# Sixteen output stores made as two halves each, and four departures of a written-out order changed, in an attention and MLP kernel on one core

## The chip, the cores and the metric

One core of one Trainium2 chip runs the kernel. The metric is the device time of one execution in microseconds; the shown time is the median of three runs. Engines are named as the profile names them: PE is the matrix engine (PEld its weight loads), DVE the vector engine, ACT the scalar engine, POOL GpSimd and SP the sync engine, which issues most of the DMAs here. Each engine runs its own list of instructions in order, and they wait for each other by semaphores.

## The reference, cut to what matters

```python
def _attn_ref(x, inducing):            # x: 4 x 12544 x 128, inducing: 32 x 128
    def mab(q, kv):
        s = scale * (q @ kv.transpose(0, 2, 1))
        s = s - s.max(-1, keepdims=True)
        a = np.exp(s)
        a /= a.sum(-1, keepdims=True) + 1e-09
        return a @ kv
    h = mab(I, x)                      # 32 rows that attend to all of x, for each batch
    return mab(x, h)                   # each row of x attends to these 32

def _moe_ref(x, w1, w2, w_out):        # 50176 x 128, 128 x 1024 twice, 1024 x 128
    h1 = x @ w1
    h2 = x @ w2
    g = np.maximum(h1, h2)
    return g @ w_out
```

The attention's output is the input of the second part. x and the output are float32, 25.7 MB each.

## The kernel before, in words

**Tiling.** A batch is cut into 98 chunks of 128 rows (`K = 98`). Row `98 p + k` of a batch lies in partition `p` of chunk `k`, so that `m` chunks that follow each other are `m` times 512 bytes in a row of memory for each partition. The four batches follow each other. For each batch the 32 pooled rows `h` are summed first (`pool_scores`, `pool_turn`, `pool_accum`, and the `small_...` functions), while the batch before is in its main part.

**Main part.** max(h1, h2) is taken as h1 + relu(h2 - h1), so one linear term and one relu term are needed. A `Block` holds up to four quarters of up to four chunks each; a quarter lives in 32 partitions. `stage` makes a block's scores (L610) and their exponentials `e`. `phase` (matmuls at L1069) sends up to four jobs at once through the four 32-row strips of PE: relu units, each one PSUM bank of 512 columns, which ACT (L1085) or DVE (L1088) then takes through the relu into SBUF, or the linear term of a group. `final_one` (L876) is one matmul of 128 columns that adds relu(h2 - h1) times `w_out` to a group's bank. A `Group` is up to four chunks of one quarter and has eight such matmuls for each chunk.

**Eviction and store.** When a group's last matmul is issued, `evict_group` multiplies the bank by the reciprocal of the softmax sums on DVE (L907) into an output tile `o`, of which there are six in turn (`outp`, `bufs=6`), and stores it at once (L935). Chunks that lie side by side go out in one DMA; four chunks are 256 KB. All stores but the last group's are issued by SP, the last one by ACT. In six groups of batch 2 (56, 60, 64, 68, 72, 76 in the order of groups) the store is already made as two DMAs of half the chunks. In the compiled program each DMA takes one of eight landing semaphores in turn, and an instruction that needs a buffer again waits for the landings of the DMAs that used it.

**SP's list.** Besides the stores, SP issues the DMA transposes of x (L172), of the pooling exponentials (L366), and, for the blocks from number 21 on, of `e` for the softmax sums (L688), which POOL then adds up (L698, L700). At the end of the program SP waits for all DMAs (L1315), and the engines leave together.

**The order.** A planner in the kernel walks through steps with a clock of its own (`Clock`) and decides at each step between a phase and a final matmul. Where the order was changed by hand, the table `DEV` names the step and the departure: 1 holds a ready phase back for one final matmul, 2 lets a phase go earlier, 3 lets a phase go ahead of column work, 4 lets column work go ahead. The table's keys are step numbers, so a change at one step shifts the meaning of the ones behind it unless they are made to fit again.

Of the kernel before, what the change touches and what calls it, by code (L numbers as in the profile page):

```python
# [102 lines left out]
def kernel(  # L103
# [93 lines left out]
    with tc.manual_schedule(engines={ET.PE, ET.DVE, ET.Activation, ET.Pool, ET.SP}):  # L197
# [585 lines left out]
        groups, ends = [], [0] * 4  # L783
# [5 lines left out]
        groups = [g for _, _, g in sorted(groups, key=lambda e: e[:2])]  # L789
# [55 lines left out]
        def linear_last(end):  # L845

            while held:
                g = held[0]
                if g.full:
                    if st[g.blk.b].get("m1r", INF) > ck.pe:  # L850
                        return
                    for s, (q, t) in enumerate(g.chunks):
                        nc.tensor.matmul(  # L853
                            out=g.ps[:, 128 * s : 128 * (s + 1)],
                            lhsT=g.blk.e2[:, 128 * t : 128 * (t + 1)],
                            rhs=m1bd[:, q, :],
                            start=False,
                            stop=True,
                            skip_group_check=True,
                        )  # L860
                    end = ck.run(0.056 * len(g.chunks))
                evict_group(held.pop(0), end)
# [30 lines left out]
        def evict_group(g, end):  # L893
            n = len(g.chunks)
            while g.blk.rp is None:
                f, a = next(job for job in pending if job[0] in DEN and job[1][0] is g.blk)
                pending.remove((f, a))
                f(*a)
            uid[0] += 1
            osb = outp.tile([128, 4, C], F32, name=f"o_{uid[0]}", tag="o")  # L900
            qs = sorted({q for q, _ in g.chunks})
            per = n // len(qs)
            t0 = g.chunks[0][1]
            rp = g.blk.rp[:, t0 : t0 + per, qs[0] : qs[-1] + 1]
            if len(qs) == 1:
                rp = rp.broadcast_to((128, per, C))
                nc.vector.tensor_mul(osb[:, 0:n, :], g.ps[:, 0 : n * C].rearrange("p (s c) -> p s c", s=n), rp)  # L907
            elif per == 1:
                rp = g.blk.rp[:, t0, qs[0] : qs[-1] + 1]
                nc.vector.tensor_mul(  # L910
                    osb[:, 0:n, :],
                    g.ps[:, 0 : n * C].rearrange("p (s c) -> p s c", s=n),
                    rp[:, :, None].broadcast_to((128, n, C)),
                )
            else:
                for i, q in enumerate(qs):
                    nc.vector.tensor_mul(
                        osb[:, per * i : per * (i + 1), :],
                        g.ps[:, per * i * C : per * (i + 1) * C].rearrange("p (s c) -> p s c", s=per),
                        g.blk.rp[:, t0 : t0 + per, q : q + 1].broadcast_to((128, per, C)),  # L920
                    )
            ck.bank[g.bank] = ck.on_dve(end, 0.066 + n * 128 / 960.0)
            runs = []
            for s, (q, t) in enumerate(g.chunks):
                qu = g.blk.quarters[q]
                c = qu.c0 + t
                if runs and runs[-1][0] == qu.b and runs[-1][1] + runs[-1][3] == c:
                    runs[-1][3] += 1
                else:
                    runs.append([qu.b, c, s, 1])  # L930
            queue = nc.scalar if g is groups[-1] else nc.sync
            for b, c, s, m in runs:
                h = m // 2 if groups.index(g) in (56, 60, 64, 68, 72, 76) else m
                for lo in range(0, m, h):
                    queue.dma_start(out=outr[b, :, c + lo : c + lo + h, :], in_=osb[:, s + lo : s + lo + h, :])  # L935
            chunks_done[0] += n
# [23 lines left out]
        def want_linear():  # L960
# [32 lines left out]
        }  # L993
        LIMIT = -16

# [324 lines left out]
```

## Time and profile before

| | |
|---|---|
| median of three runs | 324.81 us (324.77, 324.81, 325.58) |
| the profiled execution | 325.08 us |
| its span, first to last instruction | 323.2 us, granted clock 1.00 |
| DMA packets | 75,016, 53.99 MB, 167 GB/s over the span |
| HBM read and written | 27.28 MB and 25.69 MB |
| SP's own longest wait | 27.8 us, a store for its eviction |

A line of a group gives the source line, the engine, the operation, what it writes and reads, its count, then busy time, mean of one, and idle time before. `L935` is line 935 of the kernel. The chain is followed back from the last instruction through what released each step; its shares are of the span. In a table of stretches each row begins with from:to in microseconds and gives an engine's busy time with its number of instructions. In a row of a DMA queue stand packets, megabytes and the time that the packets took as a share of 16 DMA engines over the stretch. A line of waits gives engine and line, whom it waited for, the sum in us, how often and the longest. Landing is counted from the issue to the completion of a DMA.

### The profile page before, as it was taken

What the parts mean: (1) busy time and instruction counts of PE and PEld (TensorE: products, weight loads), DVE (VectorE), ACT (ScalarE), POOL (GpSimd) and SP (SyncE); (2) the same over time, 40 slices, a digit from 0 to 9 for tenths busy, and PEclk for the clock granted to TensorE, in tenths of its full rate; (3) what the DMA queues carried; (4) which work ended last, traced back from release to release, by engine and by line L of the source; (5) the groups of instructions that cost most, each with busy time, mean ns of one, the idle gap of its engine ahead of it and who ended that gap; (6) DMA issues with size and microseconds to landing.
All of it is one profiled execution on the core that took longest, in us unless ns stands there. A gap on an engine that the chain in (4) does not pass through costs nothing.

```text
span 323.2 us, 12580 instructions
## 1 busy us (share of the span) xinstructions
PE 315.9 (98%) x5375; PEld 240.1 (74%) x5375; DVE 281.3 (87%) x508; ACT 281.7 (87%) x561; POOL 37.8 (12%) x90
## 2 busy tenths in 40 slices
PE   7899999999999999999999999999999999999995
PEld 3776777777777777777777777777777777777785
DVE  3369999988989998999989999988989999899973
ACT  3789999998978999999898999998879999999960
POOL 7470000000040000000040000000006300402000
PEclk9999999999999999999999999999999999999999
DMA  8999999975279999894289999693324312323232
GB/s 205 207 267 213 226 247 199 204 137 130 99 161 243 221 249 210 161 206 145 100 163 240 232 245 191 152 228 111 118 99 109 138 67 100 125 99 116 100 115 100
DMA packets 75016, 53.99 MB, mean 167 GB/s; under 512 B 55856, under 2 KB 60624, under 8 KB 74960
## 3 DMA queue, kind: packets, MB, share of 16 engines
q1 hardware_dynamic: 68928, 39.42, 50.2%
q0 software_dynamic: 5888, 13.70, 21.7%
q8 instruction: 42, 0.69, 0.9%
q14 instruction: 14, 0.11, 0.1%
q10 hardware_dynamic: 144, 0.07, 0.1%
HBM read 27.28 MB, written 25.69 MB: 164 GB/s over the span
## 4 chain that ended last, share of the span: by engine, by line
PE 92%; DMA 5%; ACT 1%; issue 1%; POOL 0%; DVE 0%; POOLq 0%
PE ps L876 62%; PE ps L1069 22%; DMA xn<-in_x_dram 5%; PE ps L610 2%; PE ps L385 2%; PE ps L329 1%; PE ps L671 1%; PE ps L833 1%; ACT e L629 0%; PE ps L505 0%; ACT hwd L482 0%; PE ps L235 0%; PE ps L303 0%; PE ps L430 0%; PE ps L258 0%
## 5 line engine op out<-in xcount | busy, mean ns | idle before, releaser
L1085 ACT ACTIVATE relu<-ps 128x512 f16<-128x512 f32 x462 | 244.1, 605 | 23.0 <-PE ps L1069 15.0
L1088 DVE TENSOR_SCALAR relu<-ps 128x512 f16<-128x512 f32 x322 | 205.9, 681 | 16.3 <-PE ps L1069 15.0
L876 PE MATMUL ps<-woutp,relu 128*128 128x128 f16 x3136 | 216.8, 220 | 0.0
L876 PEld LDWEIGHTS <-relu 128*128 128x128 f16 x3136 | 176.6, 98 | 39.5 <-issue 28.9
L1069 PE MATMUL ps<-e,hwd 32*128 32x512 f16 (+2 forms) x888 | 88.2, 358 | 0.1
L907 DVE TENSOR_TENSOR o<-ps,rp 128x512 f32<-128x512 f32 (+3 forms) x80 | 51.1, 639 | 1.8 <-PE ps L876 1.3
L1069 PEld LDWEIGHTS <-hwd 32*128 32x128 f16 x888 | 24.5, 91 | 20.9 <-issue 0.8
L1069 PE MATMUL ps<-m,e 32*128 32x128 f16 x381 | 38.7, 217 | 0.0
L1069 PEld LDWEIGHTS <-e 32*128 32x128 f16 x381 | 21.2, 92 | 2.9 <-issue 0.4
L907 DVE TENSOR_TENSOR o<-ps,rpt 128x512 f32<-128x512 f32 (+3 forms) x28 | 17.3, 617 | 4.1 <-PE ps L853 2.2
L166 POOL DMA_DIRECT2D xn<-in_x_dram x33 | 17.9, 553 | 6.5 <-DMA xn<-in_x_dram 4.4
L164 POOL COPY pace<-hacc 128x1 f32<-128x1 f32 x2 | 0.4, 188 | 133.0 <-DVE hacc L418 133.0
L246 DVE COPY xT<-ps 128x768 f16<-128x768 f16 (+6 forms) x11 | 4.7, 457 | 8.8 <-PE ps L235 8.8
L340 ACT ACTIVATE eu<-ps 128x512 f16<-128x512 f32 x18 | 10.9, 616 | 0.1
L629 ACT ACTIVATE e<-ps 128x512 f16<-128x512 f32 (+2 forms) x21 | 10.4, 570 | 0.2 <-PE ps L610 0.2
L235 PE MATMUL ps<-identity,xn 128*128 128x128 f16 x98 | 8.6, 228 | 1.8 <-DMA xn<-in_x_dram 1.7
L535 POOL COPY m1bd<-m 32x128 f16<-32x128 f16 x4 | 1.1, 287 | 76.7 <-DVE m L530 76.6
L249 ACT COPY xT<-ps 128x768 f16<-128x768 f16 (+5 forms) x10 | 6.5, 672 | 2.9 <-PE ps L235 2.8
L698 POOL TENSOR_TENSOR w1T<-den 128x256 f32<-128x256 f16 (+1 forms) x7 | 4.4, 631 | 38.2 <-DMA den<-e 24.8
L700 POOL TENSOR_TENSOR w1T<-w1T 128x64 f32<-128x64 f32 (+4 forms) x28 | 8.4, 301 | 2.2
L235 PEld LDWEIGHTS <-xn 128*128 128x128 f16 x98 | 6.0, 102 | 3.4 <-DMA xn<-in_x_dram 2.1
L610 PE MATMUL ps<-xT,hT 128*32 128x512 f16 (+3 forms) x114 | 8.2, 361 | 0.0
(93 smaller groups left out, 117.0 us busy)
## 6 DMA issues: line engine op xcount, KB each, us to landing
out_dram<-o SPq DMA_DIRECT2D x84, 256.0 KB, 2.4
xn<-in_x_dram POOLq DMA_DIRECT2D x24, 448.0 KB, 10.1
out_dram<-o SPq DMA_DIRECT2D x22, 128.0 KB, 2.1
wf<-in_moe_w_dram POOLq DMA_DIRECT2D x4, 256.0 KB, 6.0
xn<-in_x_dram POOLq DMA_DIRECT2D x3, 224.0 KB, 8.8
xT<-xn SPq DMA_TRANSPOSE x42, 4.0
xf<-in_x_dram SPq DMA_DIRECT2D x1, 512.0 KB, 3.6
xf<-in_x_dram SPq DMA_DIRECT2D x1, 384.0 KB, 4.1
```

The costliest lines, as they stand in the source:

```text
L166: nc.gpsimd.dma_start(out=xn_at[b, i][lo:hi, 0:n, :], in_=xr[b, lo:hi, k0 : k0 + n, :])
L235: nc.tensor.transpose(ps[:, j, :], xn_at[0, i][:, g + j, :], identity16)
L249: nc.scalar.copy(out=dst, in_=ps[:, 0:m, :])
L340: nc.scalar.activation(out=eu, in_=ps, func=AF.Exp, scale=scale, accum_out=st[b]["es"][:, u : u + 1])
L610: nc.tensor.matmul(out=ps[32 * q : 32 * (q + 1), 128 * t : 128 * (t + n)], lhsT=hq, rhs=xT[:, c : c + n, :], start=True, stop=True, tile_p ...
L629: nc.scalar.activation(out=blk.e2[:, lo:hi], in_=ps[:, lo:hi], func=AF.Exp, scale=st[0]["rs"] if blk.b == 0 else scale,)
L700: nc.gpsimd.tensor_add(acc[:, :, 0:n], acc[:, :, 0:n], acc[:, :, n : 2 * n])
L876: nc.tensor.matmul(out=g.ps[:, 128 * c : 128 * (c + 1)], lhsT=g.blk.relu[q][:, 128 * (jb * w4 + t) : 128 * (jb * w4 + t + 1)], rhs=woutp[: ...
L907: nc.vector.tensor_mul(osb[:, 0:n, :], g.ps[:, 0 : n * C].rearrange("p (s c) -> p s c", s=n), rp)
L1069: nc.tensor.matmul(**seq[i])
L1085: nc.scalar.activation(out=dst, in_=src, func=AF.Relu)
L1088: nc.vector.tensor_scalar(out=dst, in0=src, scalar1=0.0, scalar2=None, op0=ALU.max)
```

## The change

Two edits. In `evict_group` the pieces of a store are two chunks long where the store has four chunks and its group is one of the six of before or one of the groups 78 to 94; all other stores stay whole. Sixteen stores of batch 3 come out as two DMAs of 128 KB in place of one of 256 KB. In the table `DEV` the entries 1409, 1413, 1442 and 1451 go, and 1425, 1431, 1438, 1440 and 1447 come in.

```diff
             for b, c, s, m in runs:
-                h = m // 2 if groups.index(g) in (56, 60, 64, 68, 72, 76) else m
+                h = 2 if m == 4 and (groups.index(g) in (56, 60, 64, 68, 72, 76) or 78 <= groups.index(g) < 95) else m
                 for lo in range(0, m, h):
                     queue.dma_start(out=outr[b, :, c + lo : c + lo + h, :], in_=osb[:, s + lo : s + lo + h, :])
...
-            1371: 2, 1386: 1, 1390: 4, 1403: 3, 1407: 4, 1409: 1, 1413: 3, 1420: 1, 1434: 1, 1442: 1, 1451:
-            4, 1454: 1, 1461: 2, 1467: 2, 1476: 3, 1480: 1, 1486: 1, 1492: 1, 1496: 1, 1507: 1, 1521: 1,
...
+            1371: 2, 1386: 1, 1390: 4, 1403: 3, 1407: 4, 1420: 1, 1425: 1, 1431: 1, 1434: 1, 1438: 2, 1440:
+            1, 1447: 3, 1454: 1, 1461: 2, 1467: 2, 1476: 3, 1480: 1, 1486: 1, 1492: 1, 1496: 1, 1507: 1,
```

The other lines of the table are only broken anew. In the compiled program SP has 16 instructions more and DVE 9 (waits for landings); ACT, POOL and PE have as many as before. PE's order differs in three places near 153 us, which the prediction names; every other engine's work keeps its order.

10 rows, old and new, of the table DEV are left out of this document.

## The prediction

> **What bounds the kernel now.** I read the page first, then busy time by stage, then the last microseconds: waits of the sync engine (SP), time to landing, and DMA packets by queue.
>
> ```profile
> span 323.2 us, 12580 instructions
> ...
> PE 315.9 (98%) x5375; PEld 240.1 (74%) x5375; DVE 281.3 (87%) x508; ACT 281.7 (87%) x561; POOL 37.8 (12%) x90
> ...
> q8 instruction: 42, 0.69, 0.9%
> q14 instruction: 14, 0.11, 0.1%
> q10 hardware_dynamic: 144, 0.07, 0.1%
> ...
> PE 92%; DMA 5%; ACT 1%; issue 1%; POOL 0%; DVE 0%; POOLq 0%
> ```
>
> The matrix engine (PE) carries 92% of the chain that ended last. Two rows matter below: queues 8 and 14 carry no data but the engines' own code. 0.69 MB for PE's 5375 + 5375 instructions is 64 bytes each, and a fetch on queue 14 is 0.11 MB / 14, 8 KB, so 128 instructions. The busy times of the stages that the edited stores lie in, 257 to 305 us, and on both sides of it:
>
> ```profile
> 230.00:257.00 27.00, 27.00 (x494) 20.87 (x490) 24.31 (x48) 23.18 (x45) 8.66 (x24) 1.00 0.35 110
> 257.00:305.00 48.00, 48.00 (x779) 36.62 (x776) 45.32 (x78) 45.45 (x89) 5.18 (x15) 1.00 0.29 102
> 305.00:320.00 15.00, 14.56 (x265) 12.93 (x263) 10.61 (x21) 7.34 (x14) 0.00 (x0) 1.00 0.33 120
> ```
>
> Columns: length, then PE, weight loads, DVE, ACT, POOL, then clock, DMA share and GB/s. PE is busy 48.00 of 48.00 us: nothing that the stores do there can make PE faster, only slower. What is left to gain lies behind PE's last matmul. The end, from the timeline and the stores' landing times (window 318 to the end):
>
> ```profile
> 318.89 0.61 PE L876 MATMUL ps<-woutp,relu 128*128 128x128 f16 x8
> ...
> 319.10 0.79 DVE L907 TENSOR_TENSOR o<-ps,rpt 128x256 f32<-128x256 f32 x2 [0.45 <-PE ps L853]
> ...
> 319.92 0.37 ACTq L935 DMA_DIRECT2D out_dram<-o  x1
> ```
>
> ```profile
> L935 SPq DMA_DIRECT2D out_dram<-o x2: 332/332/332, 318.7 to 319.5; - x2
> L935 ACTq DMA_DIRECT2D out_dram<-o x1: 370/370/370, 319.9 to 319.9; - x1
> ...
> DMA to landing us min/median/max: 1.7/1.8/2.4
> ```
>
> ```profile
> SPq L1315 <- DMA out_dram<-o: 1.6, 2, 1.0
> ```
>
> The last store goes out on ACT's queue at 319.92 and is the only one of 64 KB among the three. The two larger ones on SP's queue land in 1.7 and 1.8 us; this one, the smallest, takes 2.4. SP waits at the end of the program for both of the last landings, 1.0 us for the longer, and only then do the engines leave. So the last store's landing sets the end, and it is 0.6 to 0.7 us slower than its neighbours. DMA packets show why (four windows: 320.80:321.12, 321.12:321.14, 321.15:321.47, 321.47:321.70):
>
> ```profile
> q10 hardware_dynamic: 132, 0.06, 64.5%
> ...
> q14 instruction: 1, 0.01, 110.3%
> q10 hardware_dynamic: 2, 0.00, 11.2%
> ...
> q10 hardware_dynamic: 1, 0.00, 0.2%
> ...
> q10 hardware_dynamic: 9, 0.00, 6.1%
> ```
>
> Queue 10 is this one store: 144 packets on the page, 9 for each of 16 DMA engines. 132 start before 321.12 and 3 more by 321.15; then none for 0.32 us; then exactly 9, one engine's whole share, one after the other. In the gap lies one packet on queue 14, a code fetch at 321.13. Its time is 110.3% of 16 engines over 0.02 us, 0.35 us. One DMA engine was given an 8 KB code page first, and the last store had to wait for it.
>
> **Whose fetch it is.** From 320.3 to 321.13 only SP moves on, with one drain of ACT beside it:
>
> ```profile
> L1315 SPq EVENT_SEMAPHORE  x6: 28/28/28, 320.3 to 320.6; - x6
> ```
>
> SP's instructions between the fetch at 98.80 us (window 98.75:98.85 holds one packet of queue 14) and 321.13, first and last groups of nine:
>
> ```profile
> q14 instruction: 1, 0.01, 19.3%
> ...
> L935 SPq DMA_DIRECT2D out_dram<-o x88: 332/334/1971, 102.1 to 319.5; - x88
> L935 SPq EVENT_SEMAPHORE  x81: 17/17/17, 103.8 to 319.1; - x81
> ...
> L1315 SPq EVENT_SEMAPHORE  x7: 28/28/28, 319.9 to 320.6; - x7
> ```
>
> With the 42, 24 and 14 of the three kinds of transposes and their waits between them, the nine groups sum to 256, two pages of 128 exactly. So I read the fetch at 321.13 as SP's, and its place as a count of SP's instructions.
>
> **The change part by part, and its cost.**
>
> *Sixteen stores become two each.* Rows of the page for both sizes:
>
> ```profile
> out_dram<-o SPq DMA_DIRECT2D x84, 256.0 KB, 2.4
> ...
> out_dram<-o SPq DMA_DIRECT2D x22, 128.0 KB, 2.1
> ```
>
> Bytes stay the same. SP gets 16 more issues of 0.33 us (the store rows above), 5.3 us in all, in a stage of 48 us in which it waits 26.1 us for evictions:
>
> ```profile
> SPq L935 <- DVE o L907: 26.1, 12, 3.6
> ```
>
> The halves land about as the wholes do. Six output buffers at one store per 48/17 = 2.8 us give 17 us before a buffer is written again. Landing times of 2 to 2.4 us lie far inside that, so I take 0. Without that cover an eviction would wait the second issue, at most 0.33 us, and PE perhaps after it.
>
> *The 16 more instructions move SP's fetch.* All stand ahead of SP's last 16 instructions before 321.13. These are (window 313 to 321.13):
>
> ```profile
> L935 SPq DMA_DIRECT2D out_dram<-o x5: 332/332/333, 313.8 to 319.5; - x5
> L935 SPq EVENT_SEMAPHORE  x4: 17/17/17, 314.2 to 319.1; - x4
> ```
>
> with the 7 waits at L1315 above, 16 together. So the page ends in front of the store at 313.8, behind the one at 312.2, and the fetch should start about 0.5 us after the wait between them (as 321.13 stands to the last wait at 320.6): near 313 us. There it delays at most a share of the store of 312.2 by 0.35 us; that store's buffer is next needed, six evictions on, by the last eviction, whose group starts at 319.10. Cost 0. The last store then finds all 16 DMA engines free. The gain: at least the fetch's 0.35 us, at most 2.4 - 1.7 = 0.7. All nine packets of the late engine came behind the fetch, so without it they run beside the others', which had all started by 321.15; I take the upper part, 0.65 us.
>
> [...]
>
> *DVE gets 9 more waits.* An eviction that reuses a split buffer now waits for two landings, which takes 9 more wait instructions in the compiled list of DVE. Before, from 190 to 238 us, where six stores are split already, and from 257 to 305:
>
> ```profile
> L907 DVEq EVENT_SEMAPHORE  x17: 21/21/50, 190.5 to 235.6; - x17
> L907 DVE TENSOR_TENSOR o<-ps,rp x16: 679/680/691, 191.6 to 236.2; 128x512 f32<-128x512 f32 x16
> ...
> L907 DVEq EVENT_SEMAPHORE  x17: 21/50/50, 258.5 to 303.9; - x17
> L907 DVE TENSOR_TENSOR o<-ps,rpt x17: 676/680/692, 259.1 to 304.4; 128x512 f32<-128x512 f32 x17
> ```
>
> A wait is 0.02 to 0.05 us. Evictions take 680 ns with both kinds, so the waits pass while DVE still works on the operation before. Bounds 0 and 9 x 0.05 = 0.45 us; what would be late is the next relu, and behind it PE, for DVE is busy 45.3 of 48 us. I take 0.
>
> *The departures.* PE's list keeps its 10,739 rows and every switch; near 153 us three runs of L876 change from 3, 13, 13 to 4, 11, 14 matmuls (the run of 13 between them stays):
>
> ```profile
> 152.63 0.33 PE L876 MATMUL ps<-woutp,relu 128*128 128x128 f16 x3
> ...
> 153.22 0.90 PE L876 MATMUL ps<-woutp,relu 128*128 128x128 f16 x13
> ...
> 155.54 0.90 PE L876 MATMUL ps<-woutp,relu 128*128 128x128 f16 x13
> ...
> 156.71 0.96 PE L876 MATMUL ps<-woutp,relu 128*128 128x128 f16 x14
> ```
>
> 29 matmuls before and after. One more is 0.96 - 0.90 = 0.06 us, so a phase comes 0.06 later or earlier. If a bank is late the loss is at most the 0.12 that the run of 11 is shorter; at best 0.06 of a wait goes. Value 0. Relus on ACT and DVE keep their order.
>
> *Sum.* The profiled execution took 325.08 us, its span 323.2 and 1.9 around it. 325.08 - 0.65 = 324.43. The runs shown have a median of 324.81 (324.77 to 325.58), 0.27 less; carried over, 324.81 - 0.65 = 324.16.
>
> **The rivals.**
> 1. *No gain.* [...] Time 324.8. Chance 0.17.
> 2. *Half.* The last store is late of itself, as the first on its queue, and only the fetch's own 0.35 us goes: 324.46. For: it is queue 10's only store. Against: 15 of 16 shares had no delay. Chance 0.15.
> 3. *Slower: DVE becomes the bound* between 257 and 305 us. The nine waits and the second landings fall into an engine with 48 - 45.3 = 2.7 us to spare, PE waits behind it, and the gain at the end is absent: 324.81 + 0.45 = 325.26; if each of 16 evictions also waits 0.33 for the second issue, 330.5. It decides only once landing reaches 17 us, or waits no longer pass behind work; the equal 680 ns speak against both. Chance 0.05.
>
> **How the numbers follow.** Forecast 324.16, chance 0.63, its own range 323.9 to 324.4. With rivals 1 and 2 the range is 323.9 to 324.95; below it lies a gain above the bound, above it rival 3. A change of over 0.3%, 0.97 us, is about what a measurement of this kernel tells from none: faster than 323.84 needs the whole 0.7 and 0.27 more, chance 0.11; slower than 325.78 needs rival 3 at more than its first price, 0.04; within, 0.85.
>
> **What would show it.** In the changed profile: no packet of queue 14 after 320 us and one near 313; queue 10's 144 packets without a hole; landing of the last store 1.7 to 1.8 us and SP's last wait 0.3 to 0.4; a span near 322.5. PE stays busy 48 of 48 us between 257 and 305. A fetch still at 321, or a hole in PE after 257, would make it wrong.

## The result, and the profile after

| | before | changed |
|---|---|---|
| median | 325.05 us, 13 runs (324.77 to 325.58) | 324.34 us, 13 runs (324.12 to 325.08) |
| ratio | | 0.9979, 95% interval 0.9971 to 0.9988 |
| profiled execution, span | 325.08, 323.2 us | 324.39, 322.5 us |

The change makes the kernel 0.21% faster, 0.7 us, clear of noise and less than the 0.3% that the prediction calls "within". The page of the profile of the changed kernel, and its busy times by stage:

```profile
span 322.5 us, 12605 instructions
...
PE 315.6 (98%) x5375; PEld 239.8 (74%) x5375; DVE 281.4 (87%) x508; ACT 281.8 (87%) x561; POOL 37.8 (12%) x90
...
q14 instruction: 14, 0.11, 0.1%
q10 hardware_dynamic: 144, 0.07, 0.1%
...
PE 93%; DMA 5%; ACT 1%; issue 1%; POOL 0%; DVE 0%; POOLq 0%
```

```profile
230.00:257.00 27.00, 27.00 (x494) 20.86 (x490) 24.33 (x48) 23.18 (x45) 8.68 (x24) 1.00 0.37 113
257.00:305.00 48.00, 48.00 (x777) 36.54 (x778) 45.34 (x78) 45.51 (x88) 5.20 (x15) 1.00 0.31 102
```

PE is busy 48.00 of 48.00 us where the sixteen stores were split, as before, and DVE 45.34 in place of 45.32 with the added waits. Nothing was won or lost there. The last run of L876 in the chains of before and of the changed kernel:

```profile
318.05 0.89 PE ps L876 x16
```

```profile
318.15 0.89 PE ps L876 x16
```

In this execution PE even ends 0.1 us later, and the span is still 0.7 us shorter. All of it lies behind PE. DMA packets by queue from 320 us to the end in the changed kernel, with the landing of the store that starts there:

```profile
q1 hardware_dynamic: 189, 0.18, 19.3%
q10 hardware_dynamic: 144, 0.07, 8.6%
...
out_dram<-o ACTq DMA_DIRECT2D x1, 64.0 KB, 1.6
```

No packet of queue 14 is left in the tail, and the last store lands in 1.6 us where it took 2.4. SP's waits for stores at the end (sum, how many, the longest) and its drains behind them:

```profile
SPq L1315 <- DMA out_dram<-o: 1.1, 3, 0.7
```

```profile
L1315 SPq DRAIN  x3: 7/7/7, 321.7 to 322.0; - x3
```

The longest, 0.7 us, is now the wait for the store before the last. The wait for the last store itself, 1.0 us before, takes 0.25: in the records SP turns to it at 321.37, and it ends at 321.62 (forecast: 0.3 to 0.4). The drains, which began at 322.4 before (row below), now begin at 321.7.

```profile
L1315 SPq DRAIN  x3: 7/7/7, 322.4 to 322.7; - x3
```

One thing is not where it was forecast. The fetch that left the tail is at 307.8 us (window 307.8 to 307.9 of the changed kernel), not near 313:

```profile
q14 instruction: 1, 0.01, 19.2%
```

### The profile page after: what moved, and what is told of

It is laid out like the page before. It is cut to its first block, busy times and chain, and to the rows that moved or that the text cites. A ratio compares the mean times of both kernels' runs of the same rounds, so it can differ in the third digit from the quotient of the medians.

```text
span 322.5 us, 12605 instructions
## 1 busy us (share of the span) xinstructions
PE 315.6 (98%) x5375; PEld 239.8 (74%) x5375; DVE 281.4 (87%) x508; ACT 281.8 (87%) x561; POOL 37.8 (12%) x90
## 4 chain that ended last, share of the span: by engine, by line
PE 93%; DMA 5%; ACT 1%; issue 1%; POOL 0%; DVE 0%; POOLq 0%
PE ps L876 62%; PE ps L1069 22%; DMA xn<-in_x_dram 5%; PE ps L610 2%; PE ps L385 2%; PE ps L329 1%; PE ps L671 1%; PE ps L833 1%; ACT e L629 0%; PE ps L505 0%; ACT hwd L482 0%; PE ps L235 0%; PE ps L303 0%; PE ps L430 0%; PE ps L258 0%
## 5 line engine op out<-in xcount | busy, mean ns | idle before, releaser
L876 PE MATMUL ps<-woutp,relu 128*128 128x128 f16 x3136 | 216.9, 220 | 0.0
L876 PEld LDWEIGHTS <-relu 128*128 128x128 f16 x3136 | 176.6, 98 | 39.4 <-issue 28.9
```

The source lines that it names most:

```text
L876: nc.tensor.matmul(out=g.ps[:, 128 * c : 128 * (c + 1)], lhsT=g.blk.relu[q][:, 128 * (jb * w4 + t) : 128 * (jb * w4 + t + 1)], rhs=woutp[: ...
```

## The experiments

Each ran beside the kernel before on one chip, in two sets of four. The theory, F: the gain is SP's code fetch leaving the last store alone, and its place is a matter of how many instructions SP has run. After the first set came a second theory, L: the order in which SP asks for the landing semaphores at the end counts as well.

### The stores alone

```diff
-                h = m // 2 if groups.index(g) in (56, 60, 64, 68, 72, 76) else m
+                h = 2 if m == 4 and (groups.index(g) in (56, 60, 64, 68, 72, 76) or 78 <= groups.index(g) < 95) else m
```

> The 16 split stores with the departures of before. Theory F (the gain is SP's code fetch, whose place follows from a count of SP's instructions, leaving the last store alone): whole gain, ratio 0.998, span about 322.5, no packet of queue 14 after 320 us, last store landing in 1.6 to 1.7 us. Rival D (the departures near 153 us carry the gain): ratio 1.000, span 323.2.

Measured 324.34 us, ratio 0.9978 (0.9970 to 0.9987), span 322.7. From 320 us to the end no packet of queue 14; the last store:

```profile
out_dram<-o ACTq DMA_DIRECT2D x1, 64.0 KB, 1.6
```

The stores carry the whole gain.

### The departures alone

```diff
-            1371: 2, 1386: 1, 1390: 4, 1403: 3, 1407: 4, 1409: 1, 1413: 3, 1420: 1, 1434: 1, 1442: 1, 1451:
+            1371: 2, 1386: 1, 1390: 4, 1403: 3, 1407: 4, 1420: 1, 1425: 1, 1431: 1, 1434: 1, 1438: 2, 1440:
...
```

> The changed departures with the stores of before. Theory F: ratio 1.000 (within 0.0005), a fetch on queue 14 at 321.1 us, last store landing in 2.4 us. Rival D: ratio 0.998.

Measured 325.06 us, ratio 0.9999 (0.9991 to 1.0008), span 323.2. Packets from 320 us on:

```profile
q10 hardware_dynamic: 144, 0.07, 7.4%
q14 instruction: 1, 0.01, 1.2%
...
out_dram<-o ACTq DMA_DIRECT2D x1, 64.0 KB, 2.3
```

With SP's list as it was, the fetch is back in the tail and the last store takes 2.3 us again. The departures are worth nothing that can be measured; rival D falls.

### All stores whole

```diff
-                h = m // 2 if groups.index(g) in (56, 60, 64, 68, 72, 76) else m
+                h = m
```

> The stores of before, but the six that are split already are made whole: SP has 6 instructions fewer, so the fetch comes 6 instructions later in its list. Theory F, with the place read from both traces (the fetch starts 1.2 us after SP's 335th instruction): that is now the wait that ran at 320.64 before, so the fetch starts near 321.8 us, after the last store's packets (to 321.25 us when undisturbed); the last store lands in 1.7 us, ratio 0.998. Rival S (smaller stores themselves make it faster, as each half lands sooner): fewer halves, so ratio 1.000 or above.

Measured 325.02 us, ratio 0.9998 (0.9990 to 1.0007): F's number was missed, and by the time alone rival S would stand. The profile says otherwise. The last store's landing (packets from 319.7 us on), and one fetch, which stands at 322.8 us, when no store is under way any more:

```profile
q14 instruction: 1, 0.01, 0.8%
...
out_dram<-o ACTq DMA_DIRECT2D x1, 64.0 KB, 1.6
```

The fetch did leave the store alone, and the store landed in 1.6 us. What took the gain is SP's list of waits at L1315 (two windows, 321.47 to 321.8 and 322.1 to 322.31):

```profile
L1315 SPq EVENT_SEMAPHORE  x5: 28/28/28, 321.5 to 321.8; - x5
...
L1315 SPq EVENT_SEMAPHORE  x2: 28/28/28, 322.1 to 322.2; - x2
L1315 SPq DRAIN  x1: 7/7/7, 322.3 to 322.3; - x1
```

In the changed kernel the first of the drains follows the last landing at 321.6 at once. Here the last landing lets SP go on at 321.5, and then it has six waits to go through that are all long fulfilled, some 0.07 us each, but 0.37 us between the last of the first window and the first of the second (321.78 and 322.15 in the records): it drains at 322.3. The reason for the first part: the DMAs of SP and ACT take eight landing semaphores in turn (numbers 108, 111, 112 and 114 to 118 in the records, 23 DMAs on each in the kernel before), and SP asks for them at the end in that order, before and in the changed kernel. Six DMAs fewer turn the order by six: the last store has the second semaphore in place of the last. The 0.37 us is taken up below.

### The halves in batch 1

```diff
-                h = m // 2 if groups.index(g) in (56, 60, 64, 68, 72, 76) else m
+                h = 2 if m == 4 and (groups.index(g) in (56, 60, 64, 68, 72, 76) or 30 <= groups.index(g) < 46) else m
```

> Sixteen more split stores, but in batch 1 (groups 30 to 45), with the departures of before and the stores of batch 3 as before. Theory F: only the count matters, so the same gain, ratio 0.998, no fetch of queue 14 after 320 us. Rival S in its form for batch 3 (halves help where DMA is quiet, behind 257 us): no gain, ratio 1.000 or above, because DMA is busiest in batch 1's part and the halves only queue there.

Measured 327.19 us, ratio 1.0063 (1.0042 to 1.0084), span 324.7. F's number was missed; rival S's, 1.000 or above, came true. But the tail is as F has it: no fetch, and the last store lands in 1.6 us. The loss is in the middle, in PE's stretch 121 to 154.2 us and its waits there:

```profile
121.00:154.20 33.20, 31.42 (x542) 22.64 (x540) 28.71 (x49) 30.01 (x65) 0.00 (x0) 1.00 0.81 170
```

```profile
PE ps L351 <- DMA xT<-xn: 1.0, 1, 1.0
...
PE ps L329 <- DMA xT<-xn: 0.8, 1, 0.8
```

In the kernel before the same 542 matmuls leave no hole:

```profile
121.00:152.00 31.00, 31.00 (x542) 22.65 (x541) 28.60 (x49) 29.64 (x65) 0.00 (x0) 1.00 0.89 190
```

SP's transposes of x for batch 2 (L172), before and here:

```profile
L172 SPq DMA_TRANSPOSE xT<-xn x14: 1226/1292/5944, 102.5 to 139.0; - x14
```

```profile
L172 SPq DMA_TRANSPOSE xT<-xn x14: 1226/1237/6197, 102.5 to 142.9; - x14
```

The last transpose is issued 3.9 us later in a list of SP that has sixteen more stores, and PE waits 1.8 us for transposes of x where it waited for none before. That the halves delayed the transposes is read from the order of SP's list; no run separates it from their bytes being moved in other pieces. So the count may be changed anywhere, but not for nothing: between 257 and 305 us SP has no transposes of x to issue.

### Eight more halves, twelve more

```diff
-                h = m // 2 if groups.index(g) in (56, 60, 64, 68, 72, 76) else m
+                h = 2 if m == 4 and (groups.index(g) in (56, 60, 64, 68, 72, 76) or 84 <= groups.index(g) < 92) else m
```

> Eight more split stores in batch 3 (groups 84 to 91) with the departures of before. Theory F+L (the fetch that follows SP's count, and the order in which SP asks for the eight landing semaphores at the end): the fetch moves 8 instructions, to near 315 us, and eight DMAs more leave every later DMA on the semaphore that it had, the last store on the one that is asked for last: whole gain, ratio 0.998, span 322.5. Rival N (the gain grows with the number of halves): half of it, 0.999.

Measured 324.24 us, ratio 0.9978 (0.9968 to 0.9988), span 322.4: the whole gain with half of the halves. The fetch stands at 315.2 us, as forecast.

The kernel with twelve has 96 in place of 92.

> Twelve more split stores (groups 84 to 95), departures of before. The fetch is as far from the end as with 16 (near 311 us), but twelve DMAs more turn the landing semaphores by four: the last store has the fourth, and SP asks for four more after it. Theory F+L: 4 x 0.07 us of the gain is lost, ratio 0.9987, span about 322.8, last store landing in 1.7 us. Theory F alone: 0.998, span 322.5. Rival N: between eight and sixteen halves, 0.9985, and better than with eight.

Measured 324.49 us, ratio 0.9981 (0.9973 to 0.9990), span 322.7, with the fetch at 311.8 us. The intervals of the two overlap, and both forecasts, 0.9987 and 0.998, lie in that of the twelve, so the ratios alone do not tell F from F+L. The profiles do: in both the last store lands in 1.6 us, and behind its landing SP has (eight more, from 321.4; twelve more, from 321.5)

```profile
L1315 SPq DRAIN  x2: 7/7/7, 321.5 to 321.6; - x2
L1315 SPq EVENT_SEMAPHORE  x1: 28/28/28, 321.5 to 321.5; - x1
```

```profile
L1315 SPq EVENT_SEMAPHORE  x5: 28/28/28, 321.6 to 321.8; - x5
L1315 SPq DRAIN  x2: 7/7/7, 321.9 to 321.9; - x2
```

one wait, or five, the last store's and the four that L asked for, and the drains come some 0.2 us later after the landing. Rival N falls: eight halves already have the whole gain, and twelve have no more.

### Eight more halves with the departures

Against the changed kernel:

```diff
-                h = 2 if m == 4 and (groups.index(g) in (56, 60, 64, 68, 72, 76) or 78 <= groups.index(g) < 95) else m
+                h = 2 if m == 4 and (groups.index(g) in (56, 60, 64, 68, 72, 76) or 84 <= groups.index(g) < 92) else m
```

> Eight more split stores as in the run with eight, with the changed departures. Theory F+L: as with eight, less the 0.02 us that PE gained between 121 and 160 us with the changed departures: 0.9978, no difference from the changed kernel that can be told. Rival N: 0.999.

Measured 324.23 us, ratio 0.9977 (0.9968 to 0.9986), span 322.4. It is not told from the changed kernel, nor from the eight without the departures.

### Eight small loads in place of halves

```diff
+    extra = [consts.tile([M, 32], F32, name=f"extra{i}") for i in range(8)]
...
+            if 84 <= groups.index(g) < 92:
+                nc.sync.dma_start(out=extra[groups.index(g) - 84], in_=inducing[:, 0:32])
             chunks_done[0] += n
```

> No store is split beyond the six of before; SP issues eight small loads (4 KB each, into tiles that nothing reads) beside the stores of groups 84 to 91, so that only its count of instructions differs. Theory F+L: whole gain, 0.998, no fetch after 320 us. Rival S (halves themselves): no gain, 1.000.

Measured 324.31 us, ratio 0.9981 (0.9972 to 0.9990). From 319.9 us to the end:

```profile
q10 hardware_dynamic: 144, 0.07, 7.4%
...
out_dram<-o ACTq DMA_DIRECT2D x1, 64.0 KB, 1.6
```

Eight DMAs that serve nothing, with every store as before, give what the sixteen halves give. Rival S falls: it is the count. (In this profiled execution the span is 322.9 us at a granted clock of 0.994; the gain stands in the runs, and in the tail below.)

**The ten tails side by side.** The tail can be read in every trace without the noise of the 320 us ahead of it: the start of the fetch that comes next after SP's 335th recorded instruction, the time from the last store's issue to its landing, and from that issue to the last instruction of the program.

| kernel | fetch at, us | issue to landing, us | issue to the end, us |
|---|---|---|---|
| before | 321.13 | 2.37 | 3.30 |
| departures alone | 320.99 | 2.35 | 3.28 |
| all stores whole | 322.79 | 1.58 | 3.26 |
| twelve more halves | 311.80 | 1.59 | 2.75 |
| the changed kernel | 307.84 | 1.59 | 2.52 |
| stores alone | 307.95 | 1.60 | 2.51 |
| halves in batch 1 | 309.79 | 1.60 | 2.52 |
| eight more halves | 315.16 | 1.59 | 2.52 |
| the same with the departures | 315.14 | 1.60 | 2.52 |
| eight small loads | 315.73 | 1.59 | 2.51 |

Where the fetch meets the last store, it lands late and the tail is long. Where it does not, the store lands in 1.6 us, and the tail is 2.5 us if SP asks for it last. With four waits behind the last store 0.2 us of the gain is lost, with six waits and the gap nearly all of it. These are single executions, but the six tails in which both conditions hold lie within 0.01 us of each other, so they tell F+L from F where the ratios did not.

## Why the prediction was right, point by point

**The place of the gain.** Forecast: behind PE's last matmul, PE's stage untouched. So it was, in every run but the one with the halves in batch 1.

**The size.** Forecast 0.65 us, measured 0.7 in the spans and 0.71 between the medians of 13 runs. The bounds were 0.35, the fetch's own time, and 0.7, by the landings 2.4 and 1.7. The store lands in 1.6 now, so it gained 0.8, and 0.1 of that went to PE's later end in this execution. The nine packets that came behind the fetch are the larger part of it, though not all: from its issue to the end of its last packet the store took 1.76 us before and 1.24 in the changed kernel, 0.5 less; the rest, 0.61 against 0.35 us, lies between the last packet and the landing, and no run shows its reason. The upper part of the range was right, its reason covers 0.5 of the 0.8. Rival 2 (half) falls: the store is the only one on queue 10 in every run, and lands in 1.6 us in all eight in which it did not meet the fetch. The time itself, 324.16, was 0.18 below the measured median because it was carried over to the median of three runs, 324.81; over 13 runs the kernel before has 325.05. The sum against the profiled execution's own time, 324.43, was nearer.

**Whose fetch.** SP's: shown by the eight loads, which add to SP's list alone (DVE, ACT and POOL have as many recorded instructions as before), and by the departures alone, which leave SP's list as long as it was. In all ten traces a fetch starts 1.0 to 1.2 us after SP's 335th recorded instruction, wherever in time that instruction lies.

**The step that failed: the count.** The prediction took the fetch at 98.80 for SP's as well, read the 256 instructions from there to 321.13 as two pages exactly, let the fetch start 0.5 us after the page's end, and put it near 313 us. It came at 307.8. Between the fetch at 98.9 and the one at 307.8 the changed kernel's SP ran, first and last group,

```profile
L935 SPq DMA_DIRECT2D out_dram<-o x96: 332/423/1624, 102.2 to 306.3; - x96
L935 SPq EVENT_SEMAPHORE  x74: 17/17/17, 103.9 to 306.6; - x74
```

170, and 80 transposes and waits for them as before: 250. Six fewer than the 256, which are the six waits at 320.3 to 320.6 that the prediction counted in. So the fetch follows the first wait at L1315, at 319.9, by 1.2 us, as it follows the wait at 306.6 by 1.2 here. The match with 256 was chance, and no run shows the fetch at 98.80 to be SP's. The conclusion held because the fetch had only to leave the tail, and at 307.8 it is as harmless there as it would have been at 313.

**What was costed at nothing.** The nine waits on DVE, the halves' second issues in batch 3 and the departures cost nothing that can be measured: busy times of the stages, and ratios 0.9978 with 16, 0.9978 with 8 and 0.9999 for the departures alone. Rival 3 did not come. The same kind of edit does cost where its cover is gone: with 16 second issues among SP's transposes the kernel was 0.63% slower.

**Hidden or not.** A fetch that is hidden would have left the time unchanged. The measurement decides otherwise: the last store landed 0.8 us later where it met the fetch (2.37 against 1.59), and the kernel took 0.7 us longer. SP's own list pauses too, 0.37 us from its 335th instruction to the next where the waits around it take 0.07; in the kernel before this lay ahead of the last landings, for which SP had to wait anyway, with all stores whole it lay behind them.

**A term that the prediction did not have.** Sixteen, like eight, keeps the turn of the eight landing semaphores. The forecast would have given twelve more halves, or six fewer, the whole gain as well; of the 0.8 us in the tail they kept 0.55 and 0.04. That the change had a multiple of eight more DMAs was luck, as far as the prediction goes.

## What to carry to other kernels

When the chain ends in a DMA, compare its landing with its neighbours' of like size (here 2.4 us beside 1.7 and 1.8), and look at what other packets the DMA engines carried in that stretch: here an 8 KB fetch came by the same engines at 321.13 us, 1.2 us behind SP's 335th recorded instruction, and its place followed SP's count in all ten traces. Eight instructions more, far from the end, moved the fetch off the last transfer, to 315.2 us; choose the number so that the end's waits stay in their order, and the place so that nothing needs the queue there. A count that comes out round is no proof of where a page ends: move it by a few and look.

## What the runs showed of the hardware

- One 8 KB fetch took 0.35 us on one DMA engine (0.59 in the run with the departures alone), but held the last store's landing up by nearly 0.8 us (2.37 and 2.35 against 1.6), in both profiled executions in which it met it.
- SP needs about 0.07 us for each wait that is already fulfilled. With the last store on the last of the eight semaphores the drains follow at once; four waits behind it cost some 0.2 us, and six with the gap cost 0.7 (2.52, 2.75 and 3.26 us from the last store's issue to the end).
- The 0.37 us gap. In the kernel with all stores whole it lies between SP's 335th recorded instruction and the next, and the kernel before has the same gap at the same count: the first wait at L1315, at 319.9, is its 335th, and the next six run from 320.3 to 320.6. In the kernels with more DMAs the 335th lies among the stores, where SP waits for DVE anyway. In every run the fetch starts 1.0 to 1.2 us behind the 335th.
- The same stands 128 instructions earlier, 8 KB if SP's take the 64 bytes each that the prediction worked out for PE's. Behind its 207th recorded instruction SP pauses for 0.35 us in all ten traces (0.03 to 0.06 behind the instructions around it), and a fetch starts 1.0 to 1.3 us after that instruction's end: at 204.9 us in the kernel before, at 196.4 with the halves in batch 1, where the 207th comes earlier. So SP stood still at two counts that lie 128 apart; that a code page ends at each of them is the author's estimate. Behind the 79th, 128 earlier again, no fetch is as near (the next comes 3.9 to 4.7 us later); why is open.
